# Long convolution and routed experts on one core: when GpSimd's indirect transfers are issued

## The chip, the core and the metric

The kernel runs on one core of a Trainium2 chip. The time is device microseconds of one execution, and the figure for a kernel is the median of its runs. Engines: PE is TensorE, DVE is VectorE, ACT is ScalarE, POOL is GpSimd, SP is SyncE, which here only issues transfers.

## The reference

```python
def _attn_ref(x, h):                      # x (8, 5056, 128), h (5056, 128)
    L = 2 * S
    Xf = np.fft.rfft(x, n=L, axis=1)
    Hf = np.fft.rfft(h, n=L, axis=0)
    return np.fft.irfft(Xf * Hf[None], n=L, axis=1)[:, :S, :]

def _moe_ref(x, w_group, w_expert, w1, w2):   # x: the 40448 rows of the above
    g_idx = np.argmax(x @ w_group, axis=1)     # 4 groups; g_w: softmax weight of the one taken
    for g in range(4):
        xg = x[g_idx == g]
        e_idx = np.argmax(xg @ w_expert[g], axis=1)   # 4 experts in a group; e_w likewise
        for e in range(4):
            rows = ...                         # the rows of expert (g, e)
            ye = np.maximum(x[rows] @ w1[g, e], 0) @ w2[g, e]   # 128 -> 1024 -> 128
            out[rows] = (g_w * e_w)[:, None] * ye
```

## The kernel before

The convolution is a transform of length 10112, written as 158 x 64, all of it matmuls. It goes over the batches in three rounds (the filter and batches 0 and 1, then 2 to 4, then 5 to 7). In a round come `stage1` (the transforms of length 158), `groups` (for each pair of frequencies a 64-point transform, the product with the filter and the inverse 64-point one, over DRAM buffers `hg`, `zd`), and, laid over the work that follows, `side` (the inverse of length 158, the gate's logits, the sorting). `side` makes the output rows in eight parts for each round. Of each part `rows` copies its rows, packed, into tiles `rw` (ACT, L798; four buffers, two a part), DVE works out where each row belongs, and `scatter` then sends 128 rows at a time to the DRAM buffer `srt`, which is sorted by expert: one indirect transfer by GpSimd, L873, 10 of them for each part of round 0 and 15 for each of the others, 320 in all. Their closures wait in the list `self.sends`.

The experts work on blocks of 512 rows of `srt`. 59 blocks (`NW_MIN`) are certain whatever the routing, and stand in the main program: blocks are begun when enough rows are certain to be in `srt`, so blocks 0 to 3 (`N0` = 4) need round 0's rows, blocks up to 33 (`NA` = 34) those of rounds 0 and 1, the rest all rows. After steps 15 and 255 of the blocks a `drain` empties `self.sends` in one go, so that the next block's load (`xr <- srt`, SP) can follow. A block has eight steps (`ffn_steps`), one for each 128 of the 1024 hidden values: three matmuls of 512 columns in `mm1` (L1383 to L1385, high and low halves of the inputs), three in `mm2` (L1401 to L1403). `PLAN` says behind which step what else is put: loads and splits of the next blocks' inputs, `"s"` for the block's output (`out_store`: transposes, a multiplication by the gate into a tile `orow`, of which there are `NROW` = 4) and `"o"` for output transfers. An output transfer is another indirect one by GpSimd, 128 rows each, L1450 in `scatter_out`: 4 a block, of which for blocks 2 to 29 two are kept in DRAM and sent later (`put`, `take`, `kept_ids`). They wait in the list `self.due`. In the trace those of the main program are `out<-orow,ids` and `out<-take,kept_ids`, those of the tail `out<-orow,sids`.

The tail (`ffn_tail`) is code behind branches, since how many blocks it takes depends on the routing: here 10 more blocks of 512 rows, 10 of 384, and 9 of 256.

The program's order is each engine's order: nothing is moved by a scheduler. Steps of `side` are laid into the main list by weights (`weave`). GpSimd works through its transfers strictly in order. Which matmul a transfer waits for is set by `self.mark`: each group of matmuls leaves its last one there, and `behind` makes the transfer wait for the one that stands there when the transfer is written:

```python
def behind(self, ins):
    if self.mark is not None:
        ...
        self.tc.add_manual_dep(ins.ins, self.mark.ins.name, info, reason="transfers are issued one by one")
```

So before, a transfer is written at fixed places of the program (`self.send()` in `stage1`, `product`, `inverse` and `side`, in the main loop behind most steps of a block, at `"o"`), whether little or much work lies between two places. In the tail transfers wait for no matmul at all: four go at once when their rows are ready.

Of the kernel before, what the change touches and what calls it, by code (L numbers as in the profile page):

```python
# [23 lines left out]
NH = S // N2  # L24
# [15 lines left out]
NW_MIN = NC  # L40
NW_MAX = (NTOK + NE * 127) // BLK
# [191 lines left out]
class Kernel:  # L233
# [5 lines left out]
    def pools(self, ctx):  # L239
# [5 lines left out]
        self.turns, self.beside, self.sends, self.mark = 0, "", [], None  # L245
# [136 lines left out]
    def stage1(self, r):  # L382
# [32 lines left out]
        def mm(k):  # L415
# [7 lines left out]
            for j in range(h * QB // 2, (h + 1) * QB // 2):  # L423
                if fold:
                    for b in range(2):
                        for c in range(2):
                            self.mark = nc.tensor.matmul(
# [4 lines left out]
                else:  # L432
                    self.mark = nc.tensor.matmul(
                        whole[:, j * 256:j * 256 + N1], lhsT=views[i][:, j * 128:j * 128 + 128], rhs=self.f,
                        start=True, stop=True,
                    )
            if h == 0:
                return
# [32 lines left out]
    def groups(self, r):  # L471
# [42 lines left out]
        def forward(p):  # L514
# [7 lines left out]
            for i, (to, of, w) in enumerate(steps):  # L522
                if i == 1 and p % 2 == 0:
                    self.mark = last
# [12 lines left out]
            if p % 2 == 1:  # L537
                self.mark = last
# [22 lines left out]
        def product(p):  # L561
# [9 lines left out]
            self.send()  # L571
# [17 lines left out]
        def inverse(p):  # L589
# [7 lines left out]
            for part in range(2):  # L597
                wt, k = (cgs[p + LP], 320 - part * 64) if p > 0 else (first[0], part * 128)
                for c in range(n):
                    for h in (0, 64):  # L600
                        self.mark = nc.tensor.matmul(  # L601
# [46 lines left out]
        def step(k):  # L648
# [28 lines left out]
            for i in range(2):  # L677
                negate(k + 2 + i)
                if k - 2 + i in back:
                    yield  # L680
                    inverse(k - 2 + i)
                    if i == 1 or len(self.sends) > 20:
                        self.send()
# [14 lines left out]
    def side(self, r):  # L698
# [27 lines left out]
        def mm(n):  # L726
# [3 lines left out]
            for u in range(nu):  # L730
                for c in (0, 64):
                    k = c * nu + u * HD
                    nc.tensor.matmul(  # L733
                        pys[q][c:c + 64, col(n, u)], lhsT=zms[q][:, n % QB, k:k + 64], rhs=self.ig[:, 0:NH],
                        start=n % QB == 0 and u == 0, stop=False, tile_position=(0, c),
                    )

        def rest(n):

            zt = zts.pop(n // 4)  # L740
            for u in range(nu):
                for q in (n // QB, n // QB + 1):
                    k = q % 2 * QB * RT
                    for c in (0, 64):
                        d = c * nu + u * HD
                        both = pys[q][c:c + 64, 0:QB * c1].rearrange("p (i u m) -> p i u m", i=QB, u=nu)[:, :, u]
                        self.mark = nc.tensor.matmul(  # L747
# [3 lines left out]
                        )  # L751
            for q in (n // QB, n // QB + 1):
                k = QB * q % 8 * c1
                nc.scalar.copy(out=self.yT[:, k:k + QB * c1], in_=pys.pop(q)[:, 0:QB * c1])  # L754

        def beside():
            if self.beside != "experts":
                self.send()

        def lump(k):  # L760
            def f():
# [9 lines left out]
                beside()  # L771
# [10 lines left out]
        def rows(i):  # L782
# [10 lines left out]
            for j in range(n):  # L793
                k = (4 * i + j) * GP
                self.mark = nc.tensor.transpose(
                    out=pt[:, j * D:(j + 1) * D], in_=self.yT[:, k:k + GP], identity=self.ident
                )
            nc.scalar.copy(  # L798
# [6 lines left out]
        def lm():  # L805
            pl = bank()
            for c in range(4):
                nc.tensor.matmul(
                    pl[32 * c:32 * c + 32, 0:nsl * GP], lhsT=self.wge, rhs=self.yT[:, c * nsl * GP:(c + 1) * nsl * GP],
                    start=True, stop=True, tile_position=(0, 32 * c),  # L810
                )
            od["lT"] = cx.tile([128, 4 * GP], F32, name="lT", bufs=1)
# [23 lines left out]
        for o in range(N2 // 8):  # L836
# [3 lines left out]
            if r < 2:  # L840
# [3 lines left out]
                at.append((t + 4.7, both(lm, lambda: rows(0), beside), False))  # L844
# [44 lines left out]
    def send(self):  # L889

        if self.sends:
            self.sends.pop(0)[1]()
# [901 lines left out]
```

## Time and profile before

| | us |
|---|---|
| median of the runs | 1722.85 |
| lowest, highest run | 1707.83, 1723.93 |
| profiled execution | 1721.78 |
| its span | 1720.1 |
| PE busy | 1627.1 (95%) |
| DVE, ACT, POOL busy | 1311.6, 1084.3, 753.7 |
| mean granted TensorE clock | 0.987 of full speed |

The profile shows one execution, taken with the hardware profiler; its span lies 1.7 us below its own time. "Busy" of an engine is the time in which an instruction of it runs. The profile names for idle time what ended it (after `<-`): another engine's instruction, a DMA, "issue" for nothing that the profile shows, "remote" for an event from outside the core's engines. Stages lie at about 0 to 690 us (transforms), 690 to 1118 (experts beside the third round's `side`), 1118 to 1441 (experts alone), 1441 to 1556, 1556 to 1648 and 1648 to 1720 (the tail's blocks of 512, 384 and 256).

### The profile page before, as it was taken

To read this page: it belongs to the slowest core of one execution; us is meant where nothing else is said; L and a number is where in the kernel's file an instruction comes from. 1 tells how busy PE (TensorE), PEld (TensorE's weight loads), DVE (VectorE), ACT (ScalarE), POOL (GpSimd) and SP (SyncE) were. 2 spreads that over 40 slices of the span, in tenths; PEclk is the share of its full clock that TensorE was granted. 3 is DMA by queue.
4 is the path that set the end of the run, shared out by engine and by line. 5 is a ranking of instruction groups with operands and counts; after the bars stand their busy time and mean duration, and the time that the engine had idled before them with its cause. 6 is when DMAs were issued, how large, how long until landed. Compare 5 with 4: busy or idle time off the path is not lost. (4 is left out here: it accounts for less than half of the span.)

```text
span 1720.1 us, 46979 instructions
## 1 busy us (share of the span) xinstructions
PE 1627.1 (95%) x16576; PEld 1259.0 (73%) x16576; DVE 1311.6 (76%) x2917; ACT 1084.3 (63%) x2145; POOL 753.7 (44%) x730
## 2 busy tenths in 40 slices
PE   8998899998899987999999999999999999999997
PEld 7667755557655555777777777787788877888987
DVE  6654588775488778688877778888788888887888
ACT  5564444444445445677777777676677777777775
POOL 1451233342364545145454446145555655334545
PEclk9999999999999999999999999999999999999999
DMA  7797577867678866676666756456955687555667
GB/s 212 240 288 219 168 243 243 260 223 209 180 218 275 256 221 197 165 173 179 179 180 158 175 152 169 113 160 201 194 156 163 169 213 205 140 141 146 160 159 173
DMA packets 403936, 330.20 MB, mean 192 GB/s; under 512 B 167708, under 2 KB 347425, under 8 KB 403672
## 3 DMA queue, kind: packets, MB, share of 16 engines
q1 hardware_dynamic: 374808, 271.01, 58.5%
q0 software_dynamic: 20608, 41.79, 7.4%
q10 hardware_dynamic: 8256, 14.10, 2.9%
q8 instruction: 139, 2.28, 0.6%
q14 instruction: 125, 1.02, 0.2%
HBM read 208.00 MB, written 96.86 MB: 177 GB/s over the span
## 5 line engine op out<-in xcount | busy, mean ns | idle before, releaser
L873 POOL DMA_INDIRECT srt<-rw,pos x320 | 331.8, 1037 | 442.9 <-issue 53.5
L1450 POOL DMA_INDIRECT out<-orow,ids x176 | 184.5, 1048 | 252.4 <-PE ptr L1403 69.0
L553 DVE TENSOR_TENSOR y<-pp,hg 128x768 f32<-128x768 f32 (+1 forms) x108 | 92.4, 855 | 88.7 <-ACT hg L543 32.4
L1450 POOL DMA_INDIRECT out<-orow,sids x92 | 96.1, 1045 | 114.1 <-DVE orow L1421 88.4
L601 PE MATMUL pp<-y,cg 64*64 64x384 f32 (+1 forms) x1504 | 125.8, 449 | 14.6 <-DVE m L553 8.3
L533 PE MATMUL pp<-st,cg 64*64 64x192 f32 (+1 forms) x1588 | 120.8, 408 | 2.3 <-issue 1.1
L445 DVE TENSOR_TENSOR st<-pp,odd 128x320 f32<-128x320 f32 x96 | 46.9, 488 | 86.6 <-ACT odd L444 70.3
L614 ACT COPY zs<-pp 128x768 f32<-128x768 f32 (+1 forms) x106 | 75.7, 714 | 53.2 <-PE pp L601 43.0
L1389 DVE SCALAR_TENSOR_TENSOR h3l<-px,h3h 128x512 fp32r<-128x512 f32 (+1 forms) x111 | 74.3, 669 | 38.3 <-ACT h3h L1388 31.9
L601 PEld LDWEIGHTS pp<-y,cg 64*64 64x64 f32 x1504 | 61.0, 134 | 57.1 <-issue 29.9
L1389 DVE SCALAR_TENSOR_TENSOR h0l<-px,h0h 128x512 fp32r<-128x512 f32 (+1 forms) x109 | 73.3, 672 | 37.5 <-ACT h0h L1388 22.3
L754 ACT COPY yT<-py 128x474 f32<-128x474 f32 (+1 forms) x96 | 44.3, 513 | 88.2 <-PE py L747 86.0
L1388 ACT ACTIVATE h0h<-px 128x512 fp32r<-128x512 f32 (+1 forms) x109 | 64.0, 587 | 55.6 <-PE px L1385 39.1
L733 PEld LDWEIGHTS py<-ig,zm 126*64 126x64 f32 x2048 | 76.6, 139 | 29.7 <-issue 18.0
L733 PE MATMUL py<-ig,zm 126*64 126x79 f32 x2048 | 86.9, 237 | 11.4 <-issue 5.5
L533 PEld LDWEIGHTS pp<-st,cg 64*64 64x64 f32 x1588 | 63.2, 134 | 44.8 <-issue 34.3
L1389 DVE SCALAR_TENSOR_TENSOR h2l<-px,h2h 128x512 fp32r<-128x512 f32 (+1 forms) x112 | 75.1, 671 | 26.5 <-ACT h2h L1388 21.2
L553 DVE TENSOR_TENSOR m<-pp,hg 128x768 f32<-128x768 f32 (+1 forms) x108 | 91.3, 846 | 0.0
L1388 ACT ACTIVATE h3h<-px 128x512 fp32r<-128x512 f32 (+1 forms) x111 | 65.4, 589 | 33.2 <-PE px L1385 14.7
L798 ACT COPY rw<-py 128x1024 uint16<-128x1024 uint16 (+1 forms) x88 | 80.8, 937 | 7.0 <-PE ptr L1402 1.6
L1388 ACT ACTIVATE h1h<-px 128x512 fp32r<-128x512 f32 (+1 forms) x111 | 65.3, 588 | 29.8 <-PE px L1385 13.2
L585 POOL TENSOR_TENSOR y<-y,m 128x512 f32<-128x512 f32 x40 | 50.9, 1276 | 74.5 <-DMA hd<-hg 40.8
(478 smaller groups left out, 5129.1 us busy)
## 6 DMA issues: line engine op xcount, KB each, us to landing
wr<-in_moe_w SPq DMA_DIRECT2D x373, 256.0 KB
zd<-zs SPq DMA_DIRECT2D x66, 384.0 KB
zm<-zd SPq DMA_DIRECT2D x64, 378.0 KB
cg<-in_c_g SPq DMA_DIRECT2D x106, 224.0 KB
zd<-zs SPq DMA_DIRECT2D x39, 256.0 KB
hg<-hd SPq DMA_DIRECT2D x68, 128.0 KB
xt<-in_x ACTq DMA_DIRECT2D x52, 160.0 KB
zm<-zd SPq DMA_DIRECT2D x32, 252.0 KB
```

The costliest lines, as they stand in the source:

```text
L445: nc.vector.tensor_tensor(out=all_st[:, 0:2 * HALF, d], in0=even, in1=odd, op=ALU.add)
L533: last = nc.tensor.matmul(px[c * 64:c * 64 + 64, b, to], lhsT=k, rhs=data[:, of], start=begin, stop=i == len(steps) - 1 or p == 0 and i == ...
L553: nc.vector.tensor_tensor(out=t[:, :, 0:w].rearrange("p t (r u d) -> p t r u d", r=2, u=nu), in0=taken(px, part).unsqueeze(1).broadcast_to ...
L585: (nc.gpsimd if r == 0 else nc.vector).tensor_tensor(out=y[:, :, 0:w], in0=y[:, :, 0:w], in1=m[:, :, 0:w], op=ALU.add)
L601: self.mark = nc.tensor.matmul(pz[c][h:h + 64, 0:w], lhsT=wt[c * 64:c * 64 + 64, k + h:k + h + 64], rhs=y[c * 64:c * 64 + 64, part, 0:w], ...
L614: nc.scalar.copy(out=z[:, 0:n, 0:w], in_=pp[:, 0:n, 0:w])
L733: nc.tensor.matmul(pys[q][c:c + 64, col(n, u)], lhsT=zms[q][:, n % QB, k:k + 64], rhs=self.ig[:, 0:NH], start=n % QB == 0 and u == 0, stop ...
L798: nc.scalar.copy(out=od["rw"][i // 2][:, 4 * i % RH:4 * i % RH + n, 0:2 * D].rearrange("p j (h d) -> p j h d", h=2), in_=pt[:, 0:n * D].bi ...
L873: ins = self.nc.gpsimd.indirect_dma_start(out=self.srt, out_offset=bass.IndirectOffsetOnAxis(ap=k["pos"][0:p, j:j + 1], axis=0), in_=k["rw ...
L1388: nc.scalar.activation(out=hh, in_=p, func=AF.Relu)
L1389: nc.vector.scalar_tensor_tensor(out=hl, in0=p, scalar=0.0, in1=hh.bitcast(F32), op0=ALU.max, op1=ALU.subtract)
L1450: ins = self.nc.gpsimd.indirect_dma_start(out=self.a["out"], out_offset=bass.IndirectOffsetOnAxis(ap=ids, axis=0), in_=o, in_offset=None, ...
```

## The change

The fixed places are taken out. A clock is reckoned while the program is written: after each group of matmuls `worked` adds the time that these should take (`COL`, `COLR` us a column), leaves the last of them in `self.mark`, and, when the clock has reached `self.next`, writes one transfer, the one of the two lists that has been ready longest. A row counts as ready 1.4 reckoned us (`READY`) after it was handed over. `issued` then sets `self.next` by the pace: before the experts begin a gap of 1.9 us, or of 1.4 when more than 4 transfers wait; beside the experts 1.9, or 1.6 when more than 8 wait; never under 1.3. The two drains stay, and `ffn_tail` still empties `self.due` in one go. `out_store` first sends rows of a block that is three or more blocks back.

In the tail there is no clock. There `self.mark` is cleared at a branch's first step, one transfer is written at each `"o"`, and it waits for the last matmul written in this branch. Blocks of 384 get a plan of their own (`CHAIN_T`), blocks of 256 a second `"o"`.

```diff
+PACE = {False: (1.9, 1.4, 4), True: (1.9, 1.6, 8)}
+LEAST = 1.3
+READY, SPREAD = 1.4, 0.0
+COL, COLR = 4 / 2400, 1 / 2400 + 25e-6
...
-    HB: [(0, 0, 1), (0, 0, 2), (0, 1, "c"), (1, 1, 0), (1, 0, 3), (1.5, 1, "x"), (2.5, 0, "s"), (2.5, 0, "o"), (3, 0, "w")],
+    HB: [(0, 0, 1), (0, 0, 2), (0, 1, "c"), (1, 1, 0), (1, 0, 3), (1.5, 1, "x"), (2.5, 0, "s"), (2.5, 0, "o"), (3, 0, "o"), (3, 0, "w")],
...
+CHAIN_T = [a for a in CHAIN if a[2] != "o"] + [(4, 0, "o"), (5.5, 0, "o"), (7, 0, "o")]
...
             y = multiply(px, p, 0, "y", 4)
-            self.send()
             yield
...
+                self.worked(last, w * COL)
...
-        def beside():
-            if self.beside != "experts":
-                self.send()
...
-                at.append((t + 7.4, lambda o=o, s=sends: self.sends.extend((8 * r + o, f) for f in s), True))
+                at.append((t + 7.4, lambda o=o, s=sends: self.sends.extend((8 * r + o, f, self.clock + READY + SPREAD * i) for i, f in enumerate(s)), True))
...
         if self.sends:
             self.sends.pop(0)[1]()
+            self.issued()
+
+    def issued(self):
+
+        far, close, many = PACE[self.beside == "experts"]
+        gap = close if len(self.sends) + len(self.due) > many else far
+        self.next = max(min(self.next, self.clock) + gap, self.clock + LEAST)
+
+    def worked(self, ins, us):
+
+        self.mark = ins
+        self.clock += us
+        if not self.paced or self.clock < self.next:
+            return
+        ready = [x[0][2] for x in (self.sends, self.due) if x and x[0][2] <= self.clock]
+        if not ready:
+            return
+        if self.due and self.due[0][2] == min(ready):
+            self.scatter_out(1)
+        else:
+            self.send()
...
-            self.mark = nc.tensor.matmul(o, lhsT=wh[:, k:k + 128], rhs=xl, start=False, stop=True)
+            last = nc.tensor.matmul(o, lhsT=wh[:, k:k + 128], rhs=xh, start=True, stop=False)
+            self.worked(last, n * COLR)
...
+        while j is not None and any(d[3] is not None and d[3] <= j - NROW + 1 for d in self.due):
+            self.scatter_out(1)
...
-            if timed:
-                self.behind(ins)
+            self.behind(ins)
             self.no_dep("scatter_out", ins)
-        self.due = self.due[n:]
+            self.due = self.due[1:]
+            self.issued()
...
-                    if prev and j < NA - 2 and at in (4, 6):
+                    if j < NW_MIN:
                         self.put()
-                        self.send()
                     elif prev:
-                        self.scatter_out(1 if ns == 8 else 4, j < NW_MIN)
+                        self.scatter_out(1)
...
                 if i == 0:
+                    if not self.paced:
+                        self.mark = None
                     loads_a()
...
+        self.paced = False
...
-                        if r > 0 and k % 4 == 1:
-                            add(self.send)
...
-                    elif k < 8 * (NA - 2) and (k < 8 * (N0 - 2) or k % 8 not in (3, 4, 5, 6)):
-                        add(lambda: self.send())
-                    elif k >= 8 * (NA - 2) and k % 8 in (7, 0, 1, 2):
-                        add(lambda: self.scatter_out(1, True))
```

On PE, DVE, ACT and SP the order of the instructions stays, but for four small routing matmuls and eight small gate operations that swap with a neighbour. What moves is GpSimd's order and its waits. First GpSimd from the end of the first round's rows on, across the first drain and into the blocks beside the third round's `side`: before, where `srt<-rw,pos` rows are those sent to the experts and `out<-orow,ids` the experts' output:

```order
L873 DMA srt<-rw,pos 331776x260 x127
L1450 DMA out<-orow,ids 40448x128
L873 DMA srt<-rw,pos 331776x260 x3
L1450 DMA out<-orow,ids 40448x128
L873 DMA srt<-rw,pos 331776x260 x3
L1450 DMA out<-orow,ids 40448x128 x7
L873 DMA srt<-rw,pos 331776x260
L1450 DMA out<-orow,ids 40448x128
L873 DMA srt<-rw,pos 331776x260 x5
L1450 DMA out<-orow,ids 40448x128
```

The same place of GpSimd after the change:

```order
L874 DMA srt<-rw,pos 331776x260 x133
L1480 DMA out<-orow,ids 40448x128 x14
L874 DMA srt<-rw,pos 331776x260 x15
L1480 DMA out<-orow,ids 40448x128 x6
L874 DMA srt<-rw,pos 331776x260 x15
L1480 DMA out<-orow,ids 40448x128 x6
L874 DMA srt<-rw,pos 331776x260 x15
L1480 DMA out<-orow,ids 40448x128 x4
```

Two output rows that stood among the last rows of round 1 now follow them, and later the 15 rows of a part go together, between batches of 4 to 6 output rows, instead of alternating.

Second, GpSimd in the tail's first branch, of before, with what each instruction waits for in brackets (`DMASW` are earlier transfers by GpSimd, the number of a count is left open):

```order
L1592 COMPARE_AND_BRANCH
L1450 DMA out<-orow,sids 40448x128 [waits DMASW0_49,DVE_49]
L1450 DMA out<-orow,sids 40448x128 [waits DMASW1_49]
L1450 DMA out<-orow,sids 40448x128 [waits DMASW2_49]
L1450 DMA out<-orow,sids 40448x128 [waits DMASW3_49]
```

And the same branch after the change:

```order
L1623 COMPARE_AND_BRANCH
L1480 DMA out<-orow,sids 40448x128 [waits DMASW0_49,DVE_49,PE_49]
L1480 DMA out<-orow,sids 40448x128 [waits DMASW1_49,PE_49]
L1480 DMA out<-orow,sids 40448x128 [waits DMASW2_49,PE_49]
L1480 DMA out<-orow,sids 40448x128 [waits DMASW3_49,PE_49]
```

The four transfers of a block stay next to each other on GpSimd, but each now waits for a matmul of its own.

## Rows read from the trace of the kernel before

**Rows 1.** The page's busy times: us, share of the span, number of instructions.
```profile
PE 1627.1 (95%) x16576; PEld 1259.0 (73%) x16576; DVE 1311.6 (76%) x2917; ACT 1084.3 (63%) x2145; POOL 753.7 (44%) x730
```

**Rows 2.** Busy time of each engine by stage; granted clock, DMA share, GB/s last.
```profile
core 0: us, PE busy (x) PEld busy (x) DVE busy (x) ACT busy (x) POOL busy (x), PEclk, DMA share, GB/s
...
430.00:690.00 260.00, 229.26 (x3256) 148.89 (x3254) 188.39 (x427) 124.17 (x259) 124.58 (x121) 0.98 0.74 225
690.00:1118.00 428.00, 421.09 (x2900) 334.35 (x2901) 337.69 (x778) 307.31 (x549) 186.98 (x181) 0.99 0.64 164
1118.00:1441.00 323.00, 317.36 (x1426) 256.49 (x1424) 265.89 (x537) 233.33 (x418) 180.13 (x173) 0.99 0.71 185
```

**Rows 3.** PE's longest waits from 690 us on: total us, times, longest us.
```profile
PE ptr L1401 <- ACT h0h L1388: 4.1, 1, 4.1
PE ptr L1417 <- ACT oT L1406: 3.9, 4, 2.4
PE py L1383 <- issue: 1.6, 1, 1.6
```

**Rows 4.** GpSimd in order of time at two places: start, duration, [idle before].
```profile
1062.88 0.98 POOL L873 DMA_INDIRECT srt<-rw,pos  x1 [0.30 <-PE ptr L1403]
...
1073.62 0.98 POOL L873 DMA_INDIRECT srt<-rw,pos  x1 [0.31 <-issue]
1076.06 1.01 POOL L873 DMA_INDIRECT srt<-rw,pos  x1 [1.47 <-remote]
...
1220.25 1.21 POOL L1450 DMA_INDIRECT out<-take,kept_ids  x1 [4.22 <-PE px L1384]
...
1230.74 0.98 POOL L1450 DMA_INDIRECT out<-take,kept_ids  x1 [0.31 <-issue]
1233.73 0.98 POOL L1450 DMA_INDIRECT out<-take,kept_ids  x1 [2.01 <-remote]
```

**Rows 5.** Busy times around those two places, columns as in Rows 2.
```profile
1225.00:1230.00 5.00, 4.99 (x23) 3.79 (x21) 2.37 (x7) 1.30 (x3) 3.78 (x5) 1.00 1.31 284
1230.00:1235.00 5.00, 0.94 (x3) 0.52 (x3) 0.96 (x2) 1.59 (x4) 2.39 (x3) 0.94 0.49 98
1235.00:1240.00 5.00, 5.00 (x19) 3.86 (x19) 4.22 (x13) 3.39 (x8) 3.12 (x3) 0.72 0.71 223
1075.00:1080.00 5.00, 3.57 (x13) 2.91 (x14) 3.66 (x8) 2.85 (x5) 1.43 (x2) 0.74 0.14 46
```

**Rows 6.** GpSimd's transfers to `srt` on the page: busy us, mean ns, idle before.
```profile
L873 POOL DMA_INDIRECT srt<-rw,pos x320 | 331.8, 1037 | 442.9 <-issue 53.5
```

**Rows 7.** One DVE operation of the experts, 690 to 1556 us: ns min/median/max.
```profile
L1389 DVE SCALAR_TENSOR_TENSOR h0l<-px,h0h x89: 626/691/694, 705.9 to 1552.0; 128x512 fp32r<-128x512 f32 x89
```

**Rows 8.** First drain: GpSimd's last two rows for `srt`.
```profile
689.07 0.98 POOL L873 DMA_INDIRECT srt<-rw,pos  x1 [0.30 <-issue]
693.47 1.01 POOL L873 DMA_INDIRECT srt<-rw,pos  x1 [3.42 <-PE py L747]
```

**Rows 9.** First drain: SP's load of block 4's rows.
```profile
697.93 1.26 SPq L1284 DMA_TRANSPOSE xr<-srt  x1
```

**Rows 10.** First drain: ACT, which joins block 4's rows at L1333.
```profile
718.20 0.77 ACT L1333 COPY x<-xr 128x512 uint16<-128x512 uint16 x1
```

**Rows 11.** PE's waits for a copy of rows from 200 to 690 us.
```profile
PE py L733 <- ACT rw L798: 4.9, 4, 2.5
```

**Rows 12.** ACT's longest wait for a load from 200 to 690 us.
```profile
ACT ns L509 <- DMA cg<-in_c_g: 10.6, 3, 5.5
```

**Rows 13.** GpSimd where the tail begins.
```profile
1443.00 0.98 POOL L1450 DMA_INDIRECT out<-orow,ids  x1 [1.18 <-PE aux L1385]
1449.78 0.99 POOL L1450 DMA_INDIRECT out<-orow,sids  x1 [5.80 <-DVE orow L1421]
```

**Rows 14.** The tail's splits from 1556 us on: ns min/median/max; then who waited.
```profile
L1326 POOL TENSOR_TENSOR w3l<-wr,w3h x17: 1287/1302/1579, 1572.0 to 1707.8; 128x512 fp32r<-128x512 f32 x17
...
  PEld px L1385: 1.4, 4
```

More of the change, by code (lines that the diff above doesn't have):

```diff
@@ L244, in pools @@
         self.pq = self.banks.enter_context(tc.tile_pool(name="pq", bufs=4, space=PSUM))
-        self.turns, self.beside, self.sends, self.mark = 0, "", [], None
+        self.turns, self.beside, self.sends, self.due = 0, "", [], []
+        self.mark, self.paced, self.clock, self.next = None, True, 0.0, 0.0
     def share(self):
@@ L426, in mm @@
                         for c in range(2):
-                            self.mark = nc.tensor.matmul(
+                            last = nc.tensor.matmul(
                                 pp[c * 64:c * 64 + 64, b, j * 2 * HALF:(j + 1) * 2 * HALF],
@@ L432, in mm @@
                 else:
-                    self.mark = nc.tensor.matmul(
+                    last = nc.tensor.matmul(
                         whole[:, j * 256:j * 256 + N1], lhsT=views[i][:, j * 128:j * 128 + 128], rhs=self.f,
@@ L436, in mm @@
                     )
+            self.worked(last, 2 * (N1 if not fold else 2 * HALF) * COL)
             if h == 0:
@@ L536, in forward @@
                         )
-            if p % 2 == 1:
-                self.mark = last
+                self.worked(last, (to.stop - to.start) * COL)
             if r == 0:
@@ L600, in inverse @@
                     for h in (0, 64):
-                        self.mark = nc.tensor.matmul(
+                        last = nc.tensor.matmul(
                             pz[c][h:h + 64, 0:w], lhsT=wt[c * 64:c * 64 + 64, k + h:k + h + 64],
@@ L732, in mm @@
                     k = c * nu + u * HD
-                    nc.tensor.matmul(
+                    last = nc.tensor.matmul(
                         pys[q][c:c + 64, col(n, u)], lhsT=zms[q][:, n % QB, k:k + 64], rhs=self.ig[:, 0:NH],
@@ L736, in mm @@
                     )
+            self.worked(last, nu * NH * COL)
         def rest(n):
@@ L746, in rest @@
                         both = pys[q][c:c + 64, 0:QB * c1].rearrange("p (i u m) -> p i u m", i=QB, u=nu)[:, :, u]
-                        self.mark = nc.tensor.matmul(
+                        last = nc.tensor.matmul(
                             both, lhsT=zt[k:k + QB * RT, d:d + 64],
@@ L751, in rest @@
                         )
+            self.worked(last, nu * QB * NH * COL)
             for q in (n // QB, n // QB + 1):
@@ L770, in f @@
                 rest(4 * k)
-                beside()
             return f
@@ L807, in lm @@
             for c in range(4):
-                nc.tensor.matmul(
+                last = nc.tensor.matmul(
                     pl[32 * c:32 * c + 32, 0:nsl * GP], lhsT=self.wge, rhs=self.yT[:, c * nsl * GP:(c + 1) * nsl * GP],
@@ L811, in lm @@
                 )
+            self.worked(last, nsl * GP * COL)
             od["lT"] = cx.tile([128, 4 * GP], F32, name="lT", bufs=1)
@@ L843, in side @@
                 at.append((t + 3, lump(2 * o + 1), False))
-                at.append((t + 4.7, both(lm, lambda: rows(0), beside), False))
-                at.append((t + 6.4, both(lt, lambda: rows(1), beside), False))
-                at.append((t + 9.5, both(*more, beside), False))
+                at.append((t + 4.7, both(lm, lambda: rows(0)), False))
+                at.append((t + 6.4, both(lt, lambda: rows(1)), False))
+                at.append((t + 9.5, both(*more), False))
                 at += [(t + 6.5 + 5.6 * k / (NMATH + REST), advance(ops), True) for k in range(NMATH + REST)]
-                at.append((t + 12.15, lambda o=o, s=sends: self.sends.extend((8 * r + o, f) for f in s), True))
+                at.append((t + 12.15, lambda o=o, s=sends: self.sends.extend((8 * r + o, f, self.clock + READY + SPREAD * i) for i, f in enumerate(s)), True))
             else:
@@ L1432, in out_store @@
             self.puts.append((self.outd[j - PUT0], o[:, now:T]))
-        self.due += [(rows[:, t, 0:1], o[:, t, :]) for t in range(now)]
+        self.due += [(rows[:, t, 0:1], o[:, t, :], self.clock + READY, j) for t in range(now)]
     def put(self):
```

38 lines of the change are left out of this document (20 added, 18 removed).

## The prediction

> **What bounds the kernel now.** First the page's busy times: PE runs 1627.1 of 1720.1 us [rows 1], so all that a new order of transfers can win lies in the other 93 us, and in PE's clock. Then the same by stage, to see where these 93 lie: PE is idle for 30.7 of 260 us in the third quarter of the transforms, but for 6.9 of 428 and 5.6 of 323 while the experts run [rows 2], which is where most transfers of the change are moved. Then PE's waits from 690 us on, which tell what those few us are: one wait of 4.1 us, one of 2.4, then nothing above 1.6, and none that ends on a DMA [rows 3].
>
> The two long waits are not ordinary ones. Both fall where every engine stands still and GpSimd itself is released by "remote" [rows 4]: at about 1074 and 1231 us. The reader should look at what stands ahead: GpSimd had sent transfer after transfer with 0.3 us between them, nine from 1062.88 to 1073.62 and nine from 1220.25 to 1230.74, one each 1.3 us. In the 5 us before the second pause the DMA share is 1.31, nearly twice the stage's mean of 0.71 [rows 5, 2]. And behind each pause PE's granted clock falls: 0.94, then 0.72 for the next 5 us, and 0.74 behind the first [rows 5], where the stage has 0.99. The clock that had been at 2.4 GHz was at 1.2 for part of these stretches, after PE had been idle.
>
> **The change part by part.** To place the transfers I laid the change's reckoned clock over the matmuls' times in this trace and let GpSimd send each behind its new matmul, no faster than 1.3 us apart.
>
> *Pacing beside the experts.* Transfers come 1.5 to 2 us apart almost everywhere. Of runs of four or more back to back there are 46 from 1118 to 1441 us before, and none after. If the pauses come of the runs, both go. Their price: idle 2.4 + 4.1 = 6.5 us [rows 3]; clock (1 - 0.94) x 5 = 0.3, (1 - 0.72) x 5 = 1.4 and (1 - 0.74) x 5 = 1.3 [rows 5]; together 9.5 us. What speaks against it: other runs of eight and more, between the two places, show no pause, so the run alone isn't enough, and at 1231 something else was loading the queues. Bounds: 0, if the pauses have another cause, and 12.5 = 6.9 + 5.6, all of PE's idle time in these stages, with 3.0 of clock, 15.5. I take 9.5, because the two waits are the only ones of that kind and both stand at the end of a run.
>
> *The engines beside the transfers.* A transfer costs GpSimd 1.04 us [rows 6]; their number stays. Does sending slow others down? The DVE operation of the experts takes 626 to 694 ns, median 691, whether GpSimd is sending or not [rows 7]. Zero.
>
> *Order of rows for `srt` and output rows.* Who waits for a late row? For `srt` a block's load behind a drain, for output rows the tile `orow`. At the first drain the old program has nothing left to send, the new one five rows for `srt`: its reckoned clock is at 511 us where the trace is at 694. Five rows at 1.3 us: the last one starts at about 701 instead of 693.47 [rows 8], 7.6 us later. SP's load of block 4 then starts at 697.93 + 7.6 = 705.5 [rows 9], and SP's weight loads, which are written behind it, slide with it. ACT joins the block's rows at 718.20 [rows 10], still 12.7 us behind. Zero; if that cover were gone, up to 7.6 us and a fall of the clock like the 1.4 above, 9. At the second drain nothing is left over and the last row goes at the same time, 1073. At `ffn_tail` ten output rows are left instead of four, 6 x 1.3 = 8 us more of GpSimd behind 1443.00; before, GpSimd idles there for 5.8 us and the next transfer starts at 1449.78 [rows 13], so the tail's first rows go about 2 to 4 us later. Nobody waits for them soon: zero.
>
> *Pacing in the transforms.* The gap is 1.9 reckoned us, or 1.4. The reckoned clock runs slower than the true one there, so the last of a part's 10 or 15 rows goes 2 to 9 us later in round 0, 1 to 6 later in round 1, and 3 to 6 earlier in round 2 (beside the experts). A late row keeps its tile `rw`, of which there are four, two for each part. PE's waits that end on the copy into `rw` are four before, 4.9 us together [rows 11]; a part of round 0 comes only every 27 us (eight in a stage of 215), which is longer than the delay. Bounds: all 4.9 gone, and 16 parts of rounds 0 and 1 each with such a wait of 2.5, 40 us later. I take 0, nearer to the four waits that are there, and keep the rest for a rival. A further gain is possible: ACT waits 10.6 us for the loads `cg` in three places [rows 12]; thinner transfers might let them land sooner. Bounds 0 and 10.6; I take 0, since these loads are queued on SP behind others.
>
> *The tail.* The tail's transfers (4 for each block of 512 rows, 3 for one of 384, 2 for one of 256) now wait for matmuls of their branch. On GpSimd the splits of `w3` stand behind them: 17 from 1556 us on, 1.30 us each, and PE's waits for the splits of that line are 1.4 in four places, 0.35 each [rows 14]. The matmul that a transfer waits for has mostly ended when its rows are multiplied, since `orow` itself comes from PE's transposes, so nothing is late: zero. Bounds: 17 x 0.35 = 6 us either way, later where transfers hold up splits, sooner where splits no longer run against three transfers in a row. In DVE's split beside them the longest of nine is 1522 ns against a median of 542: sending is not what it runs beside, `w3l` is [rows 14], and that stays.
>
> The sum: 1721.8 - 9.5 = 1712.3 for an execution like the profiled one; this lies 1 us below the median of the runs, so 1713 against 1722.85.
>
> One rule speaks against it. By the Trainium skill, "DMA: Bandwidth & Descriptors", section "SWDGE vs HWDGE vs iDMA", transfers issued by GpSimd and those issued by SP or ACT feed different queues inside each DMA engine, which takes turns between them; a run on GpSimd's queue then doesn't stand ahead of weight loads, and spreading it wins nothing. The rows so far agree in part: no wait of PE from 690 us on ends on a DMA [rows 3], while the two pauses at the end of runs [rows 4] are not explained by it. By this rule the sum would be 1722.
>
> **The rivals.** *Nothing changes.* The transfers are hidden already: PE waits for none, DVE is not slowed, and the pauses may come of something that the profile doesn't show, or of the weights that load at the same time. For it: the runs without pause. Against it: two pauses, two ends of runs. Time: 1722, or, with pauses at other places, 1718 to 1726. That the change doesn't do what it says ends here too: where the reckoned clock lags, at 511 of 694 us, transfers in the transforms stand as far apart as before, and only the experts see a pace.
>
> *The loads gain too.* Besides the two pauses, the transforms lose ACT's late loads and PE's waits for `rw`: 9.5 + 10.6, if all of ACT's waits reach PE, and half of the 4.9, makes 22.6, so 1700. For it: the DMA share of 0.74 in the transforms [rows 2] is as high as anywhere. Against it: the transfers themselves are few there.
>
> *Slower: late rows hold up the copies.* Place: `rows` of rounds 0 and 1, where ACT must copy into an `rw` tile whose last rows haven't been sent. PE then waits for ACT, as now in four places for 1.2 us on average, 2.5 at most [rows 11]. Decides from: a delay of a part's last row longer than what is left until the tile is needed again; at 16 places of 1.2 us it is 19 us, with the two pauses staying 1741; with 2.5 it is 1762. For it: rows do go later there. Against it: delays of 1 to 9 us against parts that are 27 us apart.
>
> *Slower, small: block 4's rows are late.* 9 us at the first drain, against a cover of 12.7: with the pauses gone the same as before, with them 1731.
>
> **How the numbers follow.** Pauses gone and nothing else 0.45, 1713. Nothing changes 0.29, 1722. Loads gain too 0.16, 1700. Late copies 0.07, 1741 and up. Late block 4, 0.03, 1731. About 1%, 17 us, is what a measurement of this kernel can tell from no change (its runs lie 16 us apart). Faster by over 1%, below 1705.6: the third case and what the first loses more than its sum, 0.25. Slower by over 1%, above 1740: the late copies, and the far end of late block 4, 0.08. The rest 0.67. The range leaves out the slow copies and the far end of the third case: low 1698, a little under the third case's 1700; high 1729, which takes in the second's 1726 and 3 us of the tail's 6.
>
> **What would show it.** Right: no pause with "remote" on GpSimd beside the experts and a clock of 0.99 or 1.00 there throughout; PE's idle time from 690 to 1441 at some 6 us instead of 12.5; GpSimd's idle before each transfer at 0.5 us or more, with few at 0.3; the load of block 4 starting near 705, with ACT's join without a wait; tail stretches unchanged within a few us. Wrong: pauses at other places though transfers are spread; more `py <- ACT rw` waits before 690 us; gains in the transforms larger than beside the experts; splits `w3l` that PE waits for in the tail.

## The result, and the profile after

The changed kernel takes 1689.11 us (1685.06 to 1695.09, six runs) against 1721.31 for the kernel before beside it (1707.83 to 1726.79, six runs): a ratio of 0.9828, interval 0.9803 to 0.9853. That is faster by 32 us, below the range of 1698 to 1729 that was forecast.

One thing has to be known ahead of every number below. In the ten sets of runs, this one included, the median of the kernel before is either 1655 to 1658 us (six sets) or 1720 to 1726 us (four sets), with the same program and data. I call the first kind of set quiet and the second loud. The result is from a loud one. In a quiet one the change is worth nothing: 1.0004, interval 0.9984 to 1.0025. What makes a set loud isn't known; the number of the chip alone isn't it, since the sets of e16 (quiet) and e18 (loud) were both on chip 2.

Busy times by stage after, columns as in [rows 2]. The stages lie earlier in this trace (span 1687.3 us), so the same stretch holds a little more work:

```profile
430.00:690.00 260.00, 237.37 (x3249) 156.42 (x3247) 192.50 (x429) 129.79 (x272) 133.11 (x125) 0.95 0.77 229
690.00:1118.00 428.00, 424.19 (x2864) 339.39 (x2863) 350.28 (x800) 315.54 (x564) 194.45 (x189) 1.00 0.64 165
1118.00:1441.00 323.00, 318.90 (x1448) 262.38 (x1447) 273.56 (x548) 241.62 (x427) 173.44 (x169) 0.99 0.71 188
```

PE's waits after, from 660 us on (total us, times, longest), which answer to [rows 3]:

```profile
PE px L1405 <- DVE h0l L1414: 4.1, 1, 4.1
PE py L1405 <- issue: 2.3, 1, 2.3
PE py L750 <- issue: 2.2, 4, 0.9
```

Both pauses of [rows 4] are gone. One wait of 4.1 us is there that was not there before. GpSimd's rows show where it stands (its first and last transfers of twelve, 1.28 to 1.7 us apart, and the one behind them), and the busy times what it costs (columns as in [rows 2]):

```profile
1405.26 1.40 POOL L1480 DMA_INDIRECT out<-orow,ids  x1 [0.60 <-PE px L1409]
1406.96 0.98 POOL L1480 DMA_INDIRECT out<-orow,ids  x1 [0.30 <-issue]
...
1417.58 0.98 POOL L1480 DMA_INDIRECT out<-orow,ids  x1 [0.30 <-issue]
1420.28 0.98 POOL L1480 DMA_INDIRECT out<-orow,sids  x1 [1.73 <-remote]
```

```profile
1415.00:1420.00 5.00, 0.90 (x3) 0.61 (x3) 2.59 (x5) 1.10 (x2) 2.93 (x3) 0.75 0.61 148
1420.00:1425.00 5.00, 5.00 (x15) 3.90 (x14) 3.42 (x6) 2.90 (x6) 3.80 (x4) 0.57 0.33 89
```

This is the longest run of transfers back to back that the change leaves, the rows that `ffn_tail` sends in one go; the other stands at the first drain. A pause stands at its end, with "remote", PE busy for 0.90 of 5 us, and the granted clock at 0.75 and 0.57 (part of the time at 1.2 instead of 2.4 GHz) behind the idle time, as at the two places before.

**Where the 33 us of span come from.** PE runs the same 16576 matmuls in nearly the same order in both programs, so the time of the nth can be read in both traces. How far the changed kernel leads, at times of the trace before, worked out from all starts:

| time before, us | lead, us | what lies between |
|---|---|---|
| 125 | 0.6 | no transfers to `srt` yet |
| 185 | 4.5 | still none: they begin at 190.5 before, at 187.3 after |
| 347 | 11.2 | transforms, with round 0's rows |
| 684 | 18.9 | transforms, with round 1's rows |
| 697 | 26.2 | the stop of before at its first drain |
| 708 | 18.2 | the same stop of the changed kernel |
| 1070 | 19.9 | experts beside round 2 |
| 1091 | 24.1 | the pause of [rows 4] at 1074, gone |
| 1191 | 24.6 | experts |
| 1274 | 32.4 | the pause at 1231, gone |
| 1435 | 35.4 | experts |
| 1455 | 30.2 | the new pause, at the tail's begin |
| 1698 | 33.2 | tail |

More than half comes from the transforms, where the prediction saw nothing: 18.9 us up to 684, of which 4.5 stand ahead of the first transfer and can't be theirs, and 14.4 behind it. In two more traces of this pace in loud sets, e11 and e18 from below, these 14.4 are 17.3 and 19.3. PE's waits that end on "issue" are part of what went; first before, then after, both from 185 to 690 us:

```profile
PE pp L427 <- issue: 7.7, 17, 1.3
PE py L733 <- issue: 5.1, 10, 1.3
PE pp L601 <- issue: 4.4, 5, 1.9
PE pp L533 <- issue: 3.1, 13, 0.4
```

```profile
PE py L735 <- ACT rw L798: 7.4, 3, 3.6
PE pp L433 <- issue: 4.2, 10, 0.8
PE py L735 <- issue: 2.2, 3, 1.4
PE py L750 <- issue: 2.2, 4, 0.9
```

All such rows of before sum to 23.0 us, those of after to 12.6. Matmul by matmul, of the 14.4 us these waits make up 9.7 (20.1 against 10.4). Another 7.7 is busy time of PE, 450.0 against 442.3 us for the same 7001 matmuls, with the granted clock no higher after than before (0.972 and 0.978), and other waits take 3.0 back. Why PE is busy for longer isn't shown; its ends are modelled, so a late start can stand in the profile as busy time.

The waits for "issue" are not spread evenly. In the trace before, GpSimd and PE around 398 us:

```profile
396.98 0.98 POOL L873 DMA_INDIRECT srt<-rw,pos  x1 [8.98 <-PE pp L433]
398.26 0.98 POOL L873 DMA_INDIRECT srt<-rw,pos  x1 [0.31 <-issue]
400.15 0.98 POOL L873 DMA_INDIRECT srt<-rw,pos  x1 [0.90 <-remote]
```

```profile
398.33 0.36 PE L427 MATMUL pp<-f,xt 64*64 64x80 f32 x4 [0.47 <-issue]
399.08 0.38 PE L427 MATMUL pp<-f,xt 64*64 64x80 f32 x5 [0.39 <-issue]
399.80 0.43 PE L427 MATMUL pp<-f,xt 64*64 64x80 f32 x10 [0.35 <-issue]
```

PE stops three times for 0.35 to 0.47 us, each time within 1.6 us of the start of a transfer. Counted over the transforms, by the distance of a transfer from the one ahead of it: the number of transfers, and for each transfer PE's waits for "issue" (of 60 ns and more) that begin from 0.3 to 1.8 us behind its start (until 0.3 us into the next at the latest). The kernels of the last three columns are runs from below:

| distance, us | before (loud) | after (loud) | dense, e12 (loud) | dense, e1 (quiet) | before, e5 (quiet) |
|---|---|---|---|---|---|
| under 1.45 | 72: 169 ns | 23: 91 ns | 140: 451 ns | 164: 13 ns | 99: 0 ns |
| 1.45 to 1.7 | 16: 98 | 30: 41 | 9: 304 | 16: 79 | 19: 67 |
| 1.7 to 2.2 | 44: 98 | 57: 10 | 16: 223 | 9: 0 | 27: 0 |
| 2.2 to 3 | 38: 13 | 52: 32 | 16: 11 | 1: 0 | 28: 0 |
| over 3 | 31: 84 | 32: 61 | 19: 77 | 18: 0 | 33: 50 |

The short distances tell loud from quiet. The last row doesn't: a few long waits make it up, in a quiet trace too.

### The profile page after: what moved, and what is told of

It reads as the page before. It is cut to its first block, busy times and chain, and to the rows that moved or that the text cites. A ratio compares the mean times of both kernels' runs of the same rounds, so it can differ in the third digit from the quotient of the medians.

```text
span 1687.3 us, 47052 instructions
## 1 busy us (share of the span) xinstructions
PE 1607.9 (95%) x16576; PEld 1261.6 (75%) x16576; DVE 1316.2 (78%) x2917; ACT 1087.0 (64%) x2145; POOL 758.2 (45%) x730
## 3 DMA queue, kind: packets, MB, share of 16 engines
q14 instruction: 126, 1.03, 0.2%
## 4 chain that ended last, share of the span: by engine, by line
PE 81%; DMA 6%; DVE 6%; issue 3%; ACT 2%; SPq 1%; another core or an unknown queue 0%; ACTq 0%; POOL 0%; POOLq 0%; DVEq 0%
PE pp L538 8%; PE pp L604 6%; PE px L1405 5%; PE px L1409 5%; PE px L1407 5%; PE pz L1430 5%; PE pz L1426 5%; PE pz L1428 5%; PE py L735 4%; PE ptr L1430 3%; PE pp L433 3%; PE ptr L1426 3%; PE ptr L1428 3%; PE aux L1409 3%; PE pp L439 3%
## 5 line engine op out<-in xcount | busy, mean ns | idle before, releaser
L874 POOL DMA_INDIRECT srt<-rw,pos x320 | 336.3, 1051 | 428.7 <-PE py L794 62.0
L557 DVE TENSOR_TENSOR y<-pp,hg 128x768 f32<-128x768 f32 (+1 forms) x108 | 92.4, 855 | 75.0 <-PE pp L538 35.4
L604 PE MATMUL pp<-y,cg 64*64 64x384 f32 (+1 forms) x1504 | 122.2, 443 | 11.8 <-DVE m L557 7.4
```

The costliest lines, as they stand in the source:

```text
L557: nc.vector.tensor_tensor(out=t[:, :, 0:w].rearrange("p t (r u d) -> p t r u d", r=2, u=nu), in0=taken(px, part).unsqueeze(1).broadcast_to ...
L604: last = nc.tensor.matmul(pz[c][h:h + 64, 0:w], lhsT=wt[c * 64:c * 64 + 64, k + h:k + h + 64], rhs=y[c * 64:c * 64 + 64, part, 0:w], start ...
L874: ins = self.nc.gpsimd.indirect_dma_start(out=self.srt, out_offset=bass.IndirectOffsetOnAxis(ap=k["pos"][0:p, j:j + 1], axis=0), in_=k["rw ...
```

## The experiments

The theories, as the expectations name them: A, transfers back to back hold up PE in the transforms and stop all engines beside the experts; B, the places and the order of the transfers make the gain, not their distance; D, formed on the way, that transfers hold anybody up only in some sets.

**Dense transfers** (e1, e7, e9 in quiet sets, e12 in a loud one). The changed kernel with its pace taken away:

```diff
-PACE = {False: (1.9, 1.4, 4), True: (1.9, 1.6, 8)}
-LEAST = 1.3
+PACE = {False: (0.3, 0.3, 4), True: (0.3, 0.3, 8)}
+LEAST = 0.3
```

> The changed kernel with its gaps cut from 1.4-1.9 to 0.3 reckoned us: same places, same order of the other engines, but transfers go as soon as they are ready and stand back to back. Theory A (transfers back to back hold up PE's issue in the transforms and stop all engines beside the experts): PE's waits that end on 'issue' before 690 us go back from 11 us to over 20, pauses come back, time 1705 to 1722. Theory B (the places and the order of the transfers made the gain, not their distance): 1687 to 1693.

1655.54 us, 1.0006 of before (0.9978 to 1.0034). The two theories could not be told apart, since before took 1656.55 in this set. What was not expected: 164 of 208 transfers back to back, and PE's waits for "issue" from 185 to 690 us are 3.9 us in four places.

> The changed kernel with gaps of 0.3 reckoned us again. Where transfers hold PE up, theory A expects 1705 to 1722, theory B as the changed kernel within 5 us. Where they don't, as the changed kernel by both.

1657.67, ratio 1.0011 (0.9989 to 1.0033), quiet.

> Gaps of 0.3 reckoned us, on whatever chip comes next. If the kernel before takes some 1720 us there, theory A expects 0.99 to 1.00 of it (transfers back to back hold PE up as in the kernel before), theory B 0.98 (as the changed kernel). If before takes some 1657 us, both expect 1.00, as on the two chips so far, and the changed kernel's gain is the first chip's alone.

1658.53, ratio 1.0018 (0.9994 to 1.0043), quiet.

> Gaps of 0.3 reckoned us, beside the changed kernel on one chip. Where before takes 1655: both within 0.3% of it. Where it takes 1720: by theory A 0.99 to 1.00 of before, so 10 us or more over the changed kernel; by theory B as the changed kernel.

1969.84 us where before takes 1723.63: a ratio of 1.1402 (1.1344 to 1.1459), 280 us over the changed kernel beside it. A's expectation has the sign right and the size far too small, B's is missed. It is the same program that took 1657.67 in e7. PE's waits from 185 to 690 us in e12, then in e7:

```profile
PE pp L433 <- issue: 15.1, 30, 1.9
PE py L735 <- issue: 14.6, 29, 1.1
```

```profile
PE py L735 <- ACT rw L798: 7.0, 4, 2.8
PE pp L433 <- issue: 2.4, 2, 1.5
```

Beside the experts, e12 pauses behind its runs. One of them, eight transfers from 1511.34 on, with the busy times around its end (columns as in [rows 2]):

```profile
1511.34 1.01 POOL L1480 DMA_INDIRECT out<-orow,ids  x1 [3.04 <-PE px L1409]
...
1520.42 0.98 POOL L1480 DMA_INDIRECT out<-take,kept_ids  x1 [0.31 <-issue]
1526.92 0.98 POOL L1480 DMA_INDIRECT out<-orow,ids  x1 [5.53 <-PE px L1405]
```

```profile
1515.00:1520.00 5.00, 3.74 (x17) 2.77 (x15) 2.50 (x7) 1.11 (x2) 3.80 (x4) 1.00 0.71 215
1520.00:1525.00 5.00, 2.21 (x8) 1.92 (x9) 2.24 (x6) 2.31 (x5) 1.09 (x2) 0.81 0.23 76
1525.00:1530.00 5.00, 5.00 (x20) 3.99 (x20) 3.86 (x10) 3.56 (x7) 2.47 (x3) 0.85 0.36 73
```

From 1515 to 1525 PE, DVE and ACT all fall to about half, and the clock falls behind that. Counting runs of eight and more (less than 1.6 us from start to start) in the experts' stages, and waits of PE of 1 us and more that end within 3 us of the end of a run's last transfer: 9 of 19 runs in e12 have one (three more waits, of 7 us each, end within 4 us), none of 16 in e7, and two of three in the first trace. So in a loud set dense transfers cost much, and the order of GpSimd's transfers, which e12 shares with the changed kernel for all 644, is not what won. Their places are not the same: without the pace a transfer of the main program starts earlier by 45 to 66 matmuls (medians by kind of transfer), so that place and distance move together in e12. The same places cost nothing in e7, but no run moves the places alone in a loud set. A stands for loud sets; B falls for the order, and for the places it is open.

**The kernel before and the changed one again** (e5, e6 in one quiet set, e11 in a loud one), without an edit:

> The kernel before once more, with a trace of its own beside the others of this set. On the chip of the second set it took 1656 us, without the waits for 'issue' that its first trace shows. Theory A holds where the first trace's state is met again: 1715 to 1726, waits for 'issue' before 690 us over 20 us. If the chip of this set is like that of the second: 1650 to 1660 and under 5 us.

> The changed kernel beside the kernel before on one chip. Where transfers hold PE up: 0.98 of before, 1685 to 1695. Where they don't: 0.998 to 1.003 of before, since nothing else of the change was seen to win.

1657.62 and 1657.33 us; ratio of the changed kernel 1.0004 (0.9984 to 1.0025). The trace of before in the quiet set has 3.9 us of PE's waits for "issue" from 185 to 690 us, in four places, instead of 23.0. This parts all traces: PE's waits for "issue" from 185 to 690 us are 1.3 to 5.8 us in the fourteen of quiet sets, and 12.6 to 57.2 us in the six of loud ones. Up to 170 us, where no transfer has been sent, the loud and the quiet trace of before lie 0.2 us apart; at 684 it is 33.9. The quiet trace of before has 99 transfers back to back, more than the loud one; three of them:

```profile
390.24 0.98 POOL L873 DMA_INDIRECT srt<-rw,pos  x1 [15.47 <-PE pp L433]
391.53 0.97 POOL L873 DMA_INDIRECT srt<-rw,pos  x1 [0.30 <-issue]
392.81 0.97 POOL L873 DMA_INDIRECT srt<-rw,pos  x1 [0.30 <-PE pp L433]
```

> The changed kernel beside the kernel before on whatever chip comes next. By theory D (the gain is the first chip's, or its state's, where each engine is held up for some half a us behind many of GpSimd's transfers): 0.998 to 1.003 of before where that takes 1655, 0.98 where it takes 1720. By theory A on any chip: 0.98.

1690.16 us against 1723.63: 0.9814 (0.9771 to 0.9856). D holds: the gain comes again with a loud set, and with it the pause at the tail's begin. The changed kernel still takes 1690 here against 1657 in the quiet set: the pace wins back about half of what a loud set costs.

**Paced beside the experts alone** (e3, e8, e13, e16 quiet, e17 loud). The changed kernel, but the transforms' transfers are written where before wrote them:

```diff
-        if not self.paced or self.clock < self.next:
+        if not self.paced or self.beside != "experts" or self.clock < self.next:
             return
...
             y = multiply(px, p, 0, "y", 4)
+            self.place()
...
+    def place(self):
+        if self.beside != "experts":
+            self.send()
```

and `self.place()` likewise at the other places where before had `self.send()` or `beside()`.

> The changed kernel with the transforms' transfers written at the fixed places of before, and paced only from the experts on. Theory A: the 22 us gained before 690 us are lost and those behind it stay, 1706 to 1713. If what is gained in the transforms comes of something else: 1687 to 1695.

1662.55, ratio 1.0038 (1.0016 to 1.0061); a little over before, which is the only quiet run of this kernel that shows it.

> Paced only beside the experts, again. Where transfers hold PE up, theory A expects the 22 us before 690 us to be lost: 1706 to 1713. Where they don't, as the changed kernel within 6 us.

1659.5, ratio 1.0011 (0.9995 to 1.0026).

> Paced only beside the experts, the transforms' transfers at the fixed places of before. On a chip where before takes 1720: if pacing pays in both stretches, half to two thirds of the 33 us are lost, 1705 to 1715, with 20 us or more of waits for 'issue' before 690 us; if it pays beside the experts alone, 1688 to 1695. Where before takes 1655: within 6 us of it.

1656.92, ratio 1.0003 (0.9981 to 1.0025).

> Paced only beside the experts, on whatever chip comes next. Where before takes 1720: 1705 to 1715 if pacing pays in the transforms as well, 1688 to 1695 if beside the experts alone. Where before takes 1655: within 6 us of it.

1660.39, ratio 1.0008 (0.9987 to 1.0029).

> Paced only beside the experts, once more. Where before takes 1720: 1705 to 1715 if pacing pays in the transforms as well, 1688 to 1695 if beside the experts alone. Where before takes 1655: within 6 us of it.

1693.87 us against 1720.17: 0.9858 (0.9825 to 0.989). The time lies inside what was expected if pacing pays beside the experts alone. Measured as in the table of leads, though, the lead grows by 9.3 us from 185 to 684, where the changed kernel's grows by 14.4, although the transfers there are at the old places. They are not quite at the old waits: `self.mark` is now set by every group of matmuls, so a transfer waits for a later one than before, and 50 transfers stand back to back there instead of 72. From 684 to 1448 it grows by 21.7 us, the changed kernel's by 18.0, since the stop at the first drain is shorter here. What the transforms' own pacing is worth isn't settled: 5 us of lead at 708 and at 1435, 5 to 8 us by the ratios to before (0.9858 against 0.9828 and 0.9814), whose intervals overlap.

**GpSimd's own work between transfers** (e2, quiet). The kernel before with two fills of a spare tile behind each transfer:

```diff
             self.behind(ins)
+            self.gap()
...
+    def gap(self):
+        for _ in range(2):
+            self.nc.gpsimd.memset(self.pad, 0.0)
```

> The kernel before with 0.6 us of GpSimd's own work (two fills of a spare tile) behind each transfer, so that no two stand back to back; places and waits of before. Theory A: the waits for 'issue' before 690 us fall from 24 us to about 12, the pauses at 1074 and 1231 us go, time 1690 to 1703. Theory B: no gain, 1715 to 1730.

1794.97 us, 1.0837 of before (1.0806 to 1.0867). It tells nothing on A: the set was quiet, and with the fills GpSimd is busy for 1173.7 us instead of 753.7. On its page:

```profile
L904 POOL MEMSET pad<- 128x256 f32 x1288 | 417.0, 324 | 37.7
...
L1427 DVE TENSOR_TENSOR orow<-ptr,ids 128x512 f32<-128x512 f32 x58 | 39.8, 686 | 92.4 <-DMA out<-orow,ids 76.2
```

417 us more on GpSimd, the output rows leave late, and DVE waits 76.2 us for their tiles `orow`: the wait that takes the place of the one removed.

**The run at the tail's begin** (e4, e14 quiet, e18 loud). The changed kernel with the same fills there alone:

```diff
-        self.scatter_out(len(self.due))
+        while self.due:
+            self.scatter_out(1)
+            for _ in range(2):
+                nc.gpsimd.memset(self.pad, 0.0)
         self.paced = False
```

> The changed kernel with 0.6 us of GpSimd's own work behind each of the transfers that are sent in one go where the tail begins, the one long back-to-back run that is left in its trace, at whose end all engines stop for about 4 us. Theory A: no pause there, 1683 to 1686. If the pause has another cause: 1688 to 1691 with a pause at another place.

1657.55, ratio 1.0014 (0.9995 to 1.0032), quiet.

> The changed kernel with 0.6 us of GpSimd's own work behind each of the some ten transfers that go in one run where the tail begins. On a chip where before takes 1720: the pause behind that run goes, 4 to 6 us under the changed kernel, 1683 to 1687; if spacing them by GpSimd's own work does nothing, 1688 to 1692. Where before takes 1655: as before.

1656.21, ratio 0.9996 (0.9972 to 1.0021), quiet.

> The changed kernel with 0.6 us of GpSimd's own work behind each transfer of the run where the tail begins, once more. Where the kernel before takes 1720: 0.976 to 0.979 of it (the pause of 4 to 5 us behind that run goes), against 0.981 to 0.983 for the changed kernel. Where it takes 1655: 1.00.

1690.82 us against 1726.48: 0.9783 (0.9747 to 0.9819). The ratio lies where it was expected, but not for the reason given. Its interval overlaps both of the changed kernel's (0.9828 and 0.9814), so no time is won that these runs can tell, and the trace shows that the pause didn't go. Busy times where the fills stand (1404 to 1422 us) and behind them:

```profile
1410.00:1415.00 5.00, 5.00 (x24) 4.14 (x23) 3.74 (x8) 3.11 (x7) 3.96 (x7) 1.00 1.05 219
1415.00:1420.00 5.00, 5.00 (x26) 4.16 (x25) 4.20 (x8) 4.41 (x9) 3.96 (x9) 1.00 0.40 119
...
1435.00:1440.00 5.00, 2.49 (x6) 2.01 (x7) 4.24 (x9) 3.71 (x7) 2.17 (x3) 0.66 0.34 66
```

Beside the spaced transfers PE is busy throughout at full clock, where the changed kernel stood still. But the tail's first eight output rows, held back by them, then go back to back, and the pause stands behind those:

```profile
1424.24 0.98 POOL L1481 DMA_INDIRECT out<-orow,sids  x1 [2.02 <-DVE h2l L1415]
...
1433.22 0.98 POOL L1481 DMA_INDIRECT out<-orow,sids  x1 [0.30 <-issue]
1437.22 0.98 POOL L1481 DMA_INDIRECT out<-orow,sids  x1 [3.02 <-issue]
```

The pause follows the run to wherever that goes.

**Twice the transfers** (e10, quiet). The changed kernel sends each row of the transforms a second time, to a spare buffer; nothing of the result is changed:

```diff
+            for to in (self.srt, self.twin) if self.beside != "experts" else (self.srt,):
-                out=self.srt,
+                out=to,
```

> The changed kernel with each of the some 195 rows for srt that are sent in the transforms sent a second time, right behind the first, to a buffer that nobody reads: twice the transfers, every pair back to back. Theory A, on any chip: each second one costs what one back to back cost in the first trace, 0.17 us of PE's waits for 'issue', so some 30 us over the kernel before where that takes 1720, 0.02 of it. Theory D (only on the first chip, or in the state that it was in, do transfers hold PE up; elsewhere GpSimd's sending is free): where before takes 1655, the same within 8 us, the rows being sent 1 to 3 us later, and waits for 'issue' before 690 us under 5 us.

1724.21 us, ratio 1.0391 (1.0346 to 1.0435): 68 us over before, by neither theory's way. Of 386 transfers 329 are back to back, with 5 ns of PE's waits for "issue" each, as D expects; but rows leave so late that the copies into `rw` wait for tiles. PE's waits from 185 to 740 us:

```profile
PE py L736 <- ACT rw L799: 16.6, 5, 7.0
...
PE py L795 <- ACT rw L799: 8.1, 3, 4.6
```

The two rows that wait for `rw` make 24.7 us. This is the rival of the late copies, come true where GpSimd is given twice the work.

**The tail as before** (e15, quiet). The changed kernel without waits in the tail, with the plans of before there:

```diff
-            self.behind(ins)
+            if self.paced:
+                self.behind(ins)
...
-                        self.scatter_out(1)
+                        self.scatter_out(1 if ns == 8 else 4)
```

> The changed kernel with the tail's transfers as before: in runs of four, three and two, behind no matmul. On a chip where before takes 1720: the tail's runs are short and its engines are seldom held up in the first trace, so 1689 to 1694, at most 5 us over the changed kernel; if every back-to-back transfer cost 0.45 us, as in the set with dense transfers, some 60 of them would cost 27 us, 1716. Where before takes 1655: as before.

1658.58, ratio 1.0002 (0.9977 to 1.0027). In a quiet set it can tell nothing; what the tail's part is worth in a loud one stays open: from 1455 to 1698 the lead grows by 3.0 us in the first trace of the changed kernel and falls by 0.6 in e11's.

## Why the prediction was wrong, step by step

*The pauses, 9.5 us.* Right in the mechanism. Both went, and the lead grew by 4.2 us at the first and 7.8 over the stretch of the second, 12.0 together. Two counts beside it are wrong. The 46 runs of four or more from 1118 to 1441 us are runs of two or more (under 1.45 us from start to start); of four or more there are 19. And there are no other runs of eight and more between the two places, only one behind them, at 1250.9, so the case for the runs was better than it says. That a run need not end in a pause remains true: in e12 about half of the long ones do. e18 shows the pause behind the run in its new place too.

*The engines beside the transfers: zero, and with it pacing in the transforms: zero.* This is the step that failed. The prediction read it from the duration of a DVE operation [rows 7], whose median is 690 or 691 ns in loud and quiet traces alike, e12 among them. What a transfer costs is not in the durations of DVE or ACT but in the idle time ahead of their instructions and of PE's, booked on "issue", and in PE's busy time. Instead of zero the lead grew by 14.4 us from the first transfer to 684 us, 9.7 of it waits of PE for "issue" and 7.7 busy time, less 3.0 of other waits; the clock, no higher after, had no part in it. Beside the experts the lead grew by another 5.2 us outside the two pauses.

*First drain: zero.* Right in the sum: the lead is 18.9 us ahead of it and 18.2 behind it. The load of block 4 starts at 680.15, with the lead of 18.9 added 1 us later than before, not 7.6, and the cover held: ACT joins its rows at 699.96, 19.8 us after, against 20.3 in [rows 9, 10]. What the prediction overlooked is that the drain is itself a run with a stop behind it, in both programs: before, seven transfers from 681.35 to 689.07, after, eight from 669.11 to 678.57. In both PE stands idle in its stretch and the clock falls; two rows of before, then two of after:

```profile
680.00:690.00 10.00, 7.22 (x68) 5.34 (x68) 5.27 (x10) 3.87 (x7) 6.82 (x7) 0.91 0.65 165
690.00:700.00 10.00, 9.71 (x56) 6.94 (x58) 2.91 (x5) 4.79 (x9) 1.06 (x2) 0.75 0.47 136
```

```profile
670.00:680.00 10.00, 7.40 (x75) 5.41 (x73) 3.82 (x6) 3.56 (x7) 7.42 (x8) 1.00 0.41 120
680.00:690.00 10.00, 9.57 (x42) 7.50 (x41) 4.10 (x8) 4.76 (x9) 2.94 (x3) 0.66 0.78 207
```

*`ffn_tail`: zero.* 5 us lost. The prediction counted its ten rows as GpSimd's time that nobody waits for, and left out that they are a run back to back, the very thing that it had put a price on two paragraphs earlier.

*Late copies, and loads that gain.* Neither came. PE's waits for `rw` are 7.4 us in three places, against 4.9 in four [rows 11]. ACT's waits for `cg` grew instead of falling, against 10.6 us [rows 12]:

```profile
ACT ns L516 <- DMA cg<-in_c_g: 18.8, 4, 6.9
```

The rival that put 1700 came nearest, for a wrong reason.

*Nothing changes.* In quiet sets this is what happens. The rule of the Trainium skill, "DMA: Bandwidth & Descriptors", section "SWDGE vs HWDGE vs iDMA", by which the sum would be no gain, gives the right result there, which doesn't show that it is the reason. In loud sets it doesn't, and the trace doesn't contradict it: the waits that went end on no DMA, and the rule speaks of DMA queues alone.

*What stays open.* Why the engines are held up behind a transfer, by what path, and what makes a set loud; which part of the gain is the distance of the transfers and which their later places. Fetches of instructions are not seen to be it: the page's instruction queue q8 moves 139 packets in loud and quiet traces alike, at medians of 1.03 to 1.10 us each.

## What to carry to other kernels

Look at the idle time that ends on "issue", on all engines, and ask what GpSimd was doing in the 2 us ahead; the duration of a DVE or ACT instruction didn't show here what a neighbour cost. Where GpSimd's indirect transfers run beside small matmuls or in long runs, try spreading them: this kernel's pace of 1.4 to 1.9 reckoned us won 1.7 to 1.9% in loud sets and the opposite lost 14%; in quiet sets it cost nothing. Drains and flushes are runs too. Each of the two that the change left goes with a stop, and e18's fills did no more than move one. Give GpSimd no filler for every transfer, and don't let the rows fall behind: e2 and e10 lost 4 to 8% that way.

## What was not expected of the hardware

The same program takes 1657.67 us in one set and 1969.84 in another (e7, e12), with the instructions of DVE and ACT as long in one as in the other. In the loud sets the others start work late where GpSimd sends: DVE's waits for "issue" over 0.15 us sum to 49.7 us in 69 places in the trace of before (185 to 1440 us), and to 1.3 us in three in its quiet trace (185 to 1390, about the same work); ACT's to 53.6 in 83, and 3.4 in three. A result that is measured in one set alone would have told half of this, whichever half it was.
